# Inverting each chunk's triangular blocks alone, in blocks of 16, with the merge to 32 on TensorE

## Chip, cores, metric

One core of a Trainium2 chip, FP32 data. The metric is the device time of one execution in microseconds. Durations below come from one profiled execution of the kernel before.

## What is computed

The input is r, k, v, w, a, b for 4 batches, 8 heads, 768 time steps and 40 features. A recurrence with a 40 by 40 state per batch and head gives y:

```python
for t in range(S):
    y[:, :, t] = einsum('bhd,bhde->bhe', rt, state)
    Sa = einsum('bhde,bhe->bhd', state, at)
    state_decay = state * wt[:, :, None, :] - einsum('bhd,bhe->bhde', Sa, bt)
    state = state_decay + einsum('bhd,bhe->bhde', vt, kt)
```

y, reshaped to 3072 tokens of 320 features, goes into a mixture of 8 experts: logits of a gate, eight rounds of row and column normalization, and the weighted sum over the experts of `relu(x @ w1[e]) @ w2[e]` with 1024 hidden features.

## The kernel before, in words

**Chunks.** The 768 steps are cut into 12 chunks c of 64, for each of 4 batches b. The heads go in 4 pairs. Within a chunk the recurrence becomes products with a 64 by 64 unit triangular matrix per batch and head that has to be inverted: 32 matrices a chunk. Each is cut into two diagonal blocks of 32 by 32 (so 64 blocks a chunk) and one block off the diagonal.

**prep(c, b)** (L107 to L165) loads `inp` (L109), scans the decays on DVE into q (L114) and g (L122), forms kb and ab on POOL or DVE (L133, L139, L140), and multiplies and transposes them on PE into ll (L145) and kt (L153). Results go into one of 17 prepared sets: sx, bb, g, cc. ll's lower half goes to DRAM as `ld` (L148, L164). Each set lies in a memory pool of its own, and some sets that are not yet in use serve as input buffers in the first eight preparations.

**Inversion.** GROUPS pairs the chunks. For two chunks at a time `load_lu` fetches 128 blocks of 32 by 32 (L342), one a partition, and DVE inverts them in place: `inv_diag` for i = 1 to 7 on the four 8 by 8 blocks of each (L170, L173), then `inv_off` with contractions of up to 2048 elements (L179, L182). `finish` transposes a copy (L331) and stores both to DRAM as `ud` and `nd` (L333, L334).

**Merge to 64.** `tload(c)` fetches blocks of the inverses as td and tt (L211, L213, L217) and of ld as lg (L208). `tmat` makes the block off the diagonal: gp on PE (L226), copies on ACT (L227, L228), op on PE (L231), copies on ACT (L232, L233) into tt.

**recur(c, b)** has five steps: av and its mask f (L251, L252); xc and copies x1, c1 on ACT (L259, L265, L266); pu = tt times x1 and its mask pm (L270, L272); c2, ws, y and z (L277, L279, L281, L292); the transposition zt and the copies vz for the next chunk (L297, L299, L300). y is stored for the experts as xd (L285), and the gate's product lp (L307) follows some steps later. The chain from chunk to chunk of one batch is f, xc, pu, c2, z, zt, vz.

**The experts.** After the attention, layer 1 (L545), sums on DVE (L563), relu on ACT (L566), a low part on DVE (L569) and layer 2 (L610) run in blocks. `prep_w` (L473 to L501) loads weights `ws` and splits them into wh and wl on ACT and POOL; `prep_x` (L508 to L533) loads tokens `xs` and makes xch and xcl on DVE and ACT. From the eighth block on the order is written by hand.

**What sets the order.** The attention's steps are collected in a list `ev` with due times (five a chunk, batches 1.1 apart) and called in that order; P0, PD, T_LEAD, L_LEAD and INV_DT place the preparations, the inversion and the merge in it. A scheduler then arranges each engine's instructions by these priorities, their dependences and the buffers in the pools. Each engine and each DMA queue works in its order. Nearly all DMAs are issued by SP.

Of the kernel before, what the change touches and what calls it, by code (L numbers as in the profile page):

```python
# [28 lines left out]
def attention(ctx, tc, d, xd, ps, pq, pt, gs, lg):  # L29
    nc = tc.nc  # L30
    pin = ctx.enter_context(tc.tile_pool(name="a_in", bufs=1))
    inv = ctx.enter_context(tc.tile_pool(name="a_inv", bufs=1))
# [15 lines left out]
    sx_b, bb_b, g_b, cc_b = ([None] * NSX for _ in range(4))
    raws = {}
    for n in range(NCH * NB - NSX, NCH * NB):  # L50
        i, pool = n % NSX, sets[n - NCH * NB + NSX]
        if i in IN_SETS or i in KB_SETS:
            raw = pool.tile([128, 1508], F32, name=f"st{i}")
            raws[i] = raw
            sx_b[i] = raw[0:R2, 0:832].rearrange("r (p h x) -> r p h x", h=2, x=104)
            bb_b[i] = raw[:, 832:1248].rearrange("r (p x) -> r p x", x=104)
            g_b[i] = raw[0:R2, 1248:1504].rearrange("r (p x) -> r p x", x=64)
            cc_b[i] = raw[0:R2, 1504:1508]
            continue
        sx_b[i] = pool.tile([R2, NP, 2, 104], F32, name=f"sx{i}")  # L60
        bb_b[i] = pool.tile([128, NP, 104], F32, name=f"bb{i}")
        g_b[i] = pool.tile([R2, NP, 64], F32, name=f"g{i}")
        cc_b[i] = pool.tile([R2, NP], F32, name=f"cc{i}")
# [746 lines left out]
```

## Time and profile before

| | us |
|---|---|
| time, median of 3 runs (lowest, highest) | 1882.25 (1881.03, 1883.9) |
| span of the profiled execution | 1888.6 |
| PE busy in it | 1768.8 |
| first pu of chunk 0 | 119.55 |
| last pu of chunk 11 starts | 556.95 |
| PE busy from 120 to 563 | 405.31 |
| PE busy from 600 to 1888 | 1279.82 |

A row of the timeline gives start, duration, engine, line, operation, output and inputs, and in brackets how long the engine was idle before and what ended it. A row of the groups gives line, engine, operation, shapes and count, then busy time and mean duration in ns, then idle time before and what ended it. PE rows count passes: an FP32 product of 4 matmuls shows as x8.

### The profile page before, as it was taken

How to read it: one execution, taken by the hardware profiler on the slowest of the kernel's cores; microseconds unless marked ns; L12 is line 12 of the kernel's file. 1: busy time of each engine (PE TensorE's matmuls, PEld its weight loads, DVE VectorE, ACT ScalarE, POOL GpSimd, SP SyncE). 2: the span in 40 equal slices, each digit the busy share in tenths (PEclk: the TensorE clock that was granted, in tenths of full speed). 3: DMA queues.
4: the chain of work that ended last, by engine and by line, in shares of the span. 5: the costliest groups of instructions: out<-in, count | busy, mean ns of one | idle time of the engine just before them, and what ended most of it. 6: DMA issues, size and time to landing. Idle time of an engine off the chain costs nothing.

```text
span 1888.6 us, 31821 instructions
## 1 busy us (share of the span) xinstructions
PE 1768.8 (94%) x12035; PEld 1731.0 (92%) x12035; DVE 1397.3 (74%) x2330; ACT 854.1 (45%) x1845; POOL 876.9 (46%) x845
## 2 busy tenths in 40 slices
PE   4468989899898999999999999999999999999999
PEld 4367888889888999999999999999999999999999
DVE  7767767696579877776867777886776767777676
ACT  5346656665563444343433434345343433434342
POOL 6535445542255255371835528004462826537170
PEclk8569968988899999999999999999999999999999
DMA  8567766865642011110201102111110201111011
GB/s 191 100 133 151 151 140 134 166 137 119 147 117 70 23 51 37 37 56 19 73 21 53 52 22 74 55 33 37 37 55 19 73 19 55 37 37 56 18 37 42
DMA packets 187838, 136.26 MB, mean 72 GB/s; under 512 B 155941, under 2 KB 165285, under 8 KB 187685
## 3 DMA queue, kind: packets, MB, share of 16 engines
q1 hardware_dynamic: 184485, 128.98, 27.8%
q10 hardware_dynamic: 3200, 5.25, 1.1%
q8 instruction: 95, 1.56, 0.4%
q14 instruction: 58, 0.48, 0.1%
HBM read 113.74 MB, written 20.45 MB: 71 GB/s over the span
## 4 chain that ended last, share of the span: by engine, by line
PE 76%; DVE 7%; issue 2%; DMA 2%; POOL 1%; ACT 1%; SPq 0%; DVEq 0%; POOLq 0%; ACTq 0%
PE op L610 35%; PE p L545 32%; PE xc L259 2%; PE pu L270 1%; PE av L251 1%; PE ll L145 1%; PE c L277 1%; PE lp L307 1%; PE gp L226 1%; PE op L231 1%; DVE hl L569 1%; DVE un L182 1%; DVE gt L182 1%; PE zt L297 0%; DMA rb<-in_r_dram 0%
## 5 line engine op out<-in xcount | busy, mean ns | idle before, releaser
L545 PE MATMUL p<-xch,wh 128*128 128x384 f32 (+1 forms) x1792 | 605.0, 339 | 5.2 <-DVE cs L654 1.8
L566 ACT ACTIVATE hh<-sm 128x384 fp32r<-128x384 f32 x512 | 269.5, 526 | 726.5 <-DVE sm L563 726.5
L610 PE MATMUL op<-wh,hh 128*128 128x320 f32 x1536 | 477.4, 311 | 1.0 <-ACT hh L566 0.9
L610 PE MATMUL op<-wl,hh 128*128 128x320 f32 x1536 | 474.9, 310 | 0.0
L610 PE MATMUL op<-wh,hl 128*128 128x320 f32 x1536 | 468.1, 310 | 4.4 <-DVE hl L569 4.3
L491 POOL TENSOR_TENSOR wl<-ws,wh 128x640 fp32r<-128x640 f32 x60 | 103.3, 1721 | 608.4 <-ACT wh L489 608.2
L569 DVE SCALAR_TENSOR_TENSOR hl<-sm,hh 128x384 fp32r<-128x384 f32 x512 | 370.9, 758 | 2.8 <-ACT hh L566 2.5
L545 PEld LDWEIGHTS p<-xch,wh 128*128 128x128 f32 (+1 forms) x1792 | 337.5, 188 | 8.5 <-DVE u L563 2.7
L545 PE MATMUL p<-xcl,wh 128*128 128x384 f32 x896 | 302.8, 338 | 0.0
L545 PE MATMUL p<-xch,wl 128*128 128x384 f32 x896 | 302.2, 337 | 0.0
L610 PEld LDWEIGHTS op<-wh,hh 128*128 128x128 f32 x1536 | 290.6, 189 | 1.6 <-ACT hh L566 1.5
L610 PEld LDWEIGHTS op<-wh,hl 128*128 128x128 f32 x1536 | 287.2, 188 | 5.4 <-DVE hl L569 5.2
L610 PEld LDWEIGHTS op<-wl,hh 128*128 128x128 f32 x1536 | 291.5, 190 | 0.0
L563 DVE TENSOR_TENSOR sm<-p,u 128x384 f32<-128x384 f32 x384 | 232.8, 616 | 9.2 <-PE p L545 0.4
L545 PEld LDWEIGHTS p<-xcl,wh 128*128 128x128 f32 x896 | 168.8, 188 | 0.0
L545 PEld LDWEIGHTS p<-xch,wl 128*128 128x128 f32 x896 | 168.7, 188 | 0.0
L563 DVE TENSOR_TENSOR sm<-p,p 128x384 f32<-128x384 f32 x128 | 71.3, 557 | 130.1 <-PE p L545 76.3
L563 DVE TENSOR_TENSOR p<-p,p 128x384 f32<-128x384 f32 x128 | 71.2, 556 | 101.6 <-PE p L545 101.1
L563 DVE TENSOR_TENSOR u<-p,p 128x384 f32<-128x384 f32 x128 | 70.9, 554 | 59.3 <-PE p L545 58.0
L145 PE MATMUL ll<-ab,kb 104*128 104x128 f32 x336 | 63.4, 348 | 46.8 <-POOL ab L140 20.9
L499 POOL TENSOR_TENSOR wl<-ss,wh 128x512 fp32r<-128x512 f32 x60 | 90.7, 1512 | 33.5 <-ACT wh L496 29.3
L145 PEld LDWEIGHTS ll<-ab,kb 104*128 104x128 f32 x336 | 55.1, 249 | 51.3 <-POOL ab L140 27.1
(161 smaller groups left out, 2825.1 us busy)
## 6 DMA issues: line engine op xcount, KB each, us to landing
ws<-in_wts_dram SPq DMA_DIRECT2D x60, 832.0 KB
inp<-in_inp_dram SPq DMA_DIRECT2D x42, 521.6 KB
rb<-in_r_dram SPq DMA_DIRECT2D x48, 208.0 KB
ld<-lt ACTq DMA_DIRECT2D x40, 128.0 KB
vz<-in_v_dram SPq DMA_DIRECT2D x48, 104.0 KB
f<-in_vt_dram SPq DMA_DIRECT2D x48, 80.0 KB
xd<-y SPq DMA_DIRECT2D x96, 40.0 KB
st<-in_inp_dram SPq DMA_DIRECT2D x6, 521.6 KB
```

Of the source, the lines that this page charges most:

```text
L145: nc.tensor.matmul(ll[:, p], lhsT=kb[:, p], rhs=ab[:, p], start=True, stop=True)
L182: nc.vector.tensor_reduce(out=dst, in_=prv.rearrange("u c k r -> u c r k"), op=ALU.add, axis=AX.X)
L226: nc.tensor.matmul(gp[:, p], lhsT=lb[:, p], rhs=t1[:, p], start=True, stop=True)
L231: nc.tensor.matmul(op[:, p], lhsT=gs[:, p], rhs=t2[:, p], start=True, stop=True)
L259: nc.tensor.matmul(xc[h][:, p], lhsT=pp["sx"][:, p, h], rhs=f[:, p, h], start=True, stop=True)
L491: g.tensor_tensor(out=wl[:, 0:640], in0=raw[:, 256:896], in1=wh[:, 0:640], op=ALU.subtract)
L499: g.tensor_tensor(out=lv[:, 3:7], in0=so[:, :, 0], in1=hv[:, 3:7, 0], op=ALU.subtract)
L545: nc.tensor.matmul(o, lhsT=w_, rhs=x_, start=(j == 0), stop=(j == 3))
L563: eng.tensor_tensor(out=out, in0=x, in1=y, op=ALU.add)
L566: nc.scalar.activation(out=hh[:, f, h], in_=sm[f][:, h], func=AF.Relu)
L569: v.scalar_tensor_tensor(out=hl[:, f, h], in0=sm[f][:, h], scalar=0.0, in1=hh[:, f, h], op0=ALU.max, op1=ALU.subtract)
L610: nc.tensor.matmul(ops[i], lhsT=a[:, h, cs], rhs=w_[:, cw], start=(f == 0 and h == 0 and j == 0), stop=(last and h == 1 and j == 2))
```

## The change

Each chunk is inverted by itself, a 16 by 16 block at a time. A chunk has 128 such blocks, one a partition, so `load_lu` makes two DMAs (L182), `inv_diag` works on two 8 by 8 blocks (L159, L162), and `inv_off` is two contractions of 512 elements (L166, L169). `store_un(c)` stores the inverses and a copy that ACT transposes (`tr`) to DRAM in rows of 16 (L196), loads cl (L187), cb (L198), ca (L200) and xt (L202), and expands cl and cb on POOL to block-diagonal operands bl and bu of 128 by 8 by 128, by a product with the mask `mask_m` (bu of chunk 0 on DVE). `merge(c)` multiplies on PE: 8 products g16 (L214), a copy gg on ACT, 8 products x16 (L219), a copy on ACT into xt, two transpositions y16 (L224), a copy xx on ACT, and stores to nd (L221) and ud (L228). `tload` and `tmat` work as before.

The prepared sets are 13 in one pool. There are four input buffers of 1029 columns where there were two of 1284 besides the borrowed sets: g is scanned backwards over the same decays as q, so the second copy of the decays falls away. lt goes to DRAM in rows of 64 (L143). Other pieces of `prep`'s memory get two buffers. P0 goes from -8 to -2.5, PD from 0.75 to 1.25, and I_LAG = 0.5 and M_LAG = 0.6 place the inversion and the merge. What runs after the attention is not edited; its line numbers fall by two.

The core of the diff:

```diff
-    sets = [ctx.enter_context(tc.tile_pool(name=f"a_set{i}", bufs=1)) for i in range(NSX)]
+    sets = ctx.enter_context(tc.tile_pool(name="a_set", bufs=1))
...
-    INV = [(inv_diag, (i,)) for i in range(1, 8)] + [(inv_off, a) for a in ((0, 8, 8), (16, 8, 8), (0, 16, 8))]
+    def inv_off(i):
+        gt = gtf.rearrange("u (c r) -> u c r", r=8)
+        if i == 0:
+            contract(gt, un[:, 0:8, 0:8], lu[:, 0:8, 8:16])
+        else:
+            contract(un[:, 0:8, 8:16], gt, un[:, 8:16, 8:16])
+
+    INV = [(inv_diag, i) for i in range(1, 8)] + [(inv_off, 0), (inv_off, 1)]
+
+    def load_lu(c):
+        for j in range(2):
+            nc.sync.dma_start(out=lu[j * 64:j * 64 + 64], in_=dap(lds[c], j * 1040, (2080, 64), (64, 16), (1, 16)))
+
+    def store_un(c):
+        ud, nd = ud_b[c % 2], nd_b[c % 2]
+        cl = inv.tile([128, 128], F32, name="cl")
+        nc.sync.dma_start(out=cl, in_=dap(lds[c], 16, (64, 16), (2080, 64), (1, 16)))
+        bl = inv.tile([128, 8, 128], F32, name="bl")
+        mk = mask_m.unsqueeze(1).broadcast_to([128, 128, 8])
+        nc.gpsimd.tensor_tensor(out=bl.rearrange("k g (s m) -> k (g s) m", m=8),
+                                in0=cl.unsqueeze(2).broadcast_to([128, 128, 8]), in1=mk, op=ALU.mult)
+        tr = inv.tile([128, 16, 16], F32, name="tr")
+        nc.scalar.copy(out=tr, in_=un.rearrange("u c s -> u s c"))
+        for t, x in ((ud, un), (nd, tr)):
+            for j in range(2):
+                nc.sync.dma_start(out=dap(t, j * 528, (1024, 64), (32, 16), (1, 16)), in_=x[j * 64:j * 64 + 64])
+        cb = inv.tile([128, 128], F32, name="cb")
+        nc.sync.dma_start(out=cb, in_=dap(ud, 528, (32, 16), (1024, 64), (1, 16)))
+        ca = inv.tile([128, 8, 16], F32, name="ca")
+        nc.sync.dma_start(out=ca, in_=dap(nd, 0, (32, 16), (1024, 64), (1, 16)))
+        xt = inv.tile([128, 8, 32], F32, name="xt")
+        nc.sync.dma_start(out=xt[:, :, 16:32], in_=dap(nd, 528, (32, 16), (1024, 64), (1, 16)))
+        bu = inv.tile([128, 8, 128], F32, name="bu")
+        (nc.vector if c == 0 else nc.gpsimd).tensor_tensor(
+            out=bu.rearrange("k g (s m) -> k (g s) m", m=8),
+            in0=cb.unsqueeze(2).broadcast_to([128, 128, 8]), in1=mk, op=ALU.mult)
+        mops[c] = (bl, ca, bu, xt)
+
+    def merge(c):
+        ud, nd = ud_b[c % 2], nd_b[c % 2]
+        bl, ca, bu, xt = mops[c]
+        gp = pt.tile([128, 8, 16], F32, name="g16", tag="pt")
+        for g in range(8):
+            nc.tensor.matmul(gp[:, g], lhsT=bl[:, g], rhs=ca[:, g], start=True, stop=True)
+        gg = inv.tile([128, 8, 16], F32, name="gg")
+        nc.scalar.copy(out=gg, in_=gp)
+        xp = pt.tile([128, 8, 16], F32, name="x16", tag="pt")
+        for g in range(8):
+            nc.tensor.matmul(xp[:, g], lhsT=bu[:, g], rhs=gg[:, g], start=True, stop=True)
+        nc.scalar.copy(out=xt[:, :, 0:16], in_=xp)
+        nc.sync.dma_start(out=dap(nd, 512, (32, 16), (1024, 64), (1, 16)), in_=xt[:, :, 0:16])
+        xq = pt.tile([128, 2, 128], F32, name="y16", tag="pt")
+        for i in range(2):
+            nc.tensor.transpose(xq[:, i], xt[:, 4 * i:4 * i + 4].rearrange("a g c -> a (g c)"), ident)
+        xx = inv.tile([128, 2, 8, 16], F32, name="xx")
+        nc.scalar.copy(out=xx, in_=xq.rearrange("a i (s m) -> a i m s", m=8))
+        for i in range(2):
+            nc.sync.dma_start(out=dap(ud, i * 4096 + 16, (32, 128), (8192, 8), (1, 16)), in_=xx[:, i])
...
-P0 = -8
-PD = 0.75
+P0 = -2.5
+PD = 1.25
+I_LAG = 0.5
+M_LAG = 0.6
...
-NSX = 17
+NSX = 13
+NIN = 4
```

How the order of instructions moves, at three places. A row names line, operation, output and inputs with a buffer's number, shape and count.

On PE, before the first pu (pu_880) of the kernel before:

```order
L226 MATMUL gp_756<-td_192,lg_193 64x32 x8
L145 MATMUL ll_906<-ab0_194,kb_896 128x128 x4
L153 MATMUL kt_911<-cst_144,kb_896 128x104 x4
L231 MATMUL op_767<-td_192,lg_193 64x32 x8
L226 MATMUL gp_949<-td_192,lg_193 64x32 x8
L270 MATMUL pu_880<-x1_863,tt0_190 128x104 x4
```

and of the changed kernel (pu_799; g16_362 to y16_384 are the merge of chunk 0, g16_591 to y16_613 that of chunk 1):

```order
L214 MATMUL g16_362<-ca_356,bl_346 128x16 x8
L147 MATMUL kt_778<-cst_98,kb_761 128x104 x4
L141 MATMUL ll_898<-ab0_156,kb_888 128x128 x4
L219 MATMUL x16_373<-gg_371,bu_360 128x16 x8
L147 MATMUL kt_905<-cst_98,kb_888 128x104 x4
L224 MATMUL y16_384<-cst_98,xt_358 128x128 x2
L214 MATMUL g16_591<-ca_552,bl_542 128x16 x8
L219 MATMUL x16_602<-gg_600,bu_556 128x16 x8
L224 MATMUL y16_613<-cst_98,xt_554 128x128 x2
L256 MATMUL gp_674<-td_154,lg_155 64x32 x8
L261 MATMUL op_685<-td_154,lg_155 64x32 x8
L256 MATMUL gp_841<-td_154,lg_155 64x32 x8
```

The row after the last one is pu_799. Two merges stand ahead of it, and ll_898 is the thirteenth ll of the program, where ll_906 is the seventeenth.

On PE, where chunk 2 begins (pu_1731 is its first pu) in the kernel before:

```order
L251 MATMUL av_1705<-rb_1699,vz4_201 104x128 x4
L297 MATMUL zt_1711<-cst_144,z_1595 40x104 x4
L307 MATMUL lp_1775<-gs_65,y_1377 64x8 x2
L145 MATMUL ll_1611<-ab1_195,kb_1603 128x128 x4
L153 MATMUL kt_1616<-cst_144,kb_1603 128x104 x4
L277 MATMUL c2_1718<-pm_1644,bb7_178 104x104 x4
L270 MATMUL pu_1731<-x1_1693,tt0_190 128x104 x4
```

and in the changed kernel (pu_1740, four rows behind these; g16_1381 to y16_1403 are the merge of chunk 3, gp_1565 and op_1576 belong to chunk 2):

```order
L307 MATMUL c2_1715<-pm_1642,bb7_120 104x104 x4
L214 MATMUL g16_1381<-ca_1337,bl_1327 128x16 x8
L219 MATMUL x16_1392<-gg_1390,bu_1341 128x16 x8
L224 MATMUL y16_1403<-cst_98,xt_1339 128x128 x2
L337 MATMUL lp_1434<-gs_65,y_1034 64x8 x4
L337 MATMUL lp_1525<-gs_65,y_1151 64x8 x4
L256 MATMUL gp_1565<-td_154,lg_155 64x32 x8
L141 MATMUL ll_1601<-ab0_156,kb_1593 128x128 x4
L147 MATMUL kt_1608<-cst_98,kb_1593 128x104 x4
L261 MATMUL op_1576<-td_154,lg_155 64x32 x8
```

The merge of chunk 3 stands in one piece between the last c2 of chunk 1 and gp of chunk 2.

On DVE, the last gate copies (lg) and the first operands of the experts (xcl0, xch0) in the kernel before:

```order
L525 TENSOR_TENSOR xcl0_5550<-xs_5594,xch0_5549 128x3x128
L528 TENSOR_TENSOR xch0_5549<-xs_5594,xch0_5549 32x3x128
...
L312 COPY lg_62<-lp_5221 64x8
L531 TENSOR_TENSOR xcl0_5550<-xt_5600,xch0_5549 128x4x128
L533 TENSOR_TENSOR xch0_5549<-xt_5600,xch0_5549 32x4x128
```

and in the changed kernel (lp_6007 is the last gate product, mxs the first step behind it):

```order
L342 COPY lg_62<-lp_6007 64x8
L624 TENSOR_REDUCE mxs_6199<-lg_62 128x1
L523 TENSOR_TENSOR xcl0_6057<-xs_6101,xch0_6056 128x3x128
L526 TENSOR_TENSOR xch0_6056<-xs_6101,xch0_6056 32x3x128
L529 TENSOR_TENSOR xcl0_6057<-xt_6107,xch0_6056 128x4x128
L531 TENSOR_TENSOR xch0_6056<-xt_6107,xch0_6056 32x4x128
L523 TENSOR_TENSOR xcl0_6057<-xs_6119,xch0_6056 128x3x128
```

Before, all twelve such instructions on xcl0 and xch0 stand ahead of the last seven gate copies. Now the first of them stands behind the last gate copy. The same holds for the first cast of wh0 on ACT (before among chunk 10's and 11's copies, now behind the last x1 and c1) and for the first wl0 on POOL (now behind the last y).

More of the change, by code (lines that the diff above doesn't have):

```diff
@@ L37, in attention @@
     dr = ctx.enter_context(tc.tile_pool(name="a_dr", bufs=2, space=bass.MemoryType.DRAM))
-    cst = const.tile([128, 64 + 64 + 104 + 128 + 40 + 260], F32, name="cst")
+    dr1 = ctx.enter_context(tc.tile_pool(name="a_dr1", bufs=1, space=bass.MemoryType.DRAM))
+    cst = const.tile([128, 668], F32, name="cst")
     nc.sync.dma_start(out=cst, in_=d["cst"])
@@ L45, in attention @@
     one65 = cst[0:R2, 400:660]
+    mask_m = cst[:, 660:668]
     NTB = 2
[L48 to L63, printed above, removed]
+    sx_b = [sets.tile([R2, NP, 2, 104], F32, name=f"sx{i}") for i in range(NSX)]
+    bb_b = [sets.tile([128, NP, 104], F32, name=f"bb{i}") for i in range(NSX)]
+    g_b = [sets.tile([R2, NP, 65], F32, name=f"g{i}") for i in range(NSX)]
+    cc_b = [sets.tile([R2, NP], F32, name=f"cc{i}") for i in range(NSX)]
     tt_b = [const.tile([128, 4 * NP, 128], F32, name=f"tt{i}") for i in range(NTB)]
@@ new lines, in merge @@
+    def merge(c):
[16 more added lines that the diff above has]
+        nc.scalar.copy(out=xx, in_=xq.rearrange("a i (s m) -> a i m s", m=8))
+        for i in range(2):
+            nc.sync.dma_start(out=dap(ud, i * 4096 + 16, (32, 128), (8192, 8), (1, 16)), in_=xx[:, i])
@@ L365, in attention @@
             ev.append((t + 2 * SKEW * half, tmat, (c, half)))
-    for s, cs in enumerate(GROUPS):
-        us = slice(0, 64 * len(cs))
-        t0 = 5 * cs[0] - 10
-        n = len(cs) * NB
-        for i in range(n):
-            cb = (cs[0] + i // NB, i % NB)
-            j = cb[0] * NB + cb[1] - NSX
+        for b in range(NB):
+            j = c * NB + b - NSX
             t = 5 * (j // 4) + 3 + SKEW * (j % 4) + 0.01
-            t = max(t, t0 + P0 + PD * i) if s else -20 + 0.01 * i
-            ev.append((t, do_prep, (s,) + cb + (i == 0,)))
-        t += 0.02
-        ev.append((t, load_lu, (s, len(cs))))
+            t = max(t, 5 * (c - 2) + P0 + PD * b) if c else -20 + 0.01 * b
+            ev.append((t, prep, (c, b)))
+        t += 0.02 if c == 0 else I_LAG
+        ev.append((t, load_lu, (c,)))
         for i, (fn, a) in enumerate(INV):
-            ev.append((t + INV_DT * i, fn, (us,) + a))
-        ev.append((t + INV_DT * 10 + 0.01, finish, (s, us)))
+            ev.append((t + INV_DT * i, fn, (a,)))
+        ev.append((t + INV_DT * 9, store_un, (c,)))
+        ev.append((t + INV_DT * 9 + M_LAG * (c > 0), merge, (c,)))
     for _, fn, args in sorted(ev, key=lambda x: x[0]):
@@ L398 @@
 NRB = 2
[L399 to L403 removed]
+KB_POOL = (1, 2, 3, 4, 5, 6, 7)
 N_SP = 8
[L405 removed]
 NFAST = 6
@@ L777, in _layout @@
     gate[0:40], gate[64:104] = wg[0], wg[1]
-    cst = np.zeros((128, 660), np.float32)
+    cst = np.zeros((128, 668), np.float32)
     i = np.arange(64)
@@ L788, in _layout @@
     cst[64:104, 360:400] = np.eye(40)
-    cst[:, 400::65] = 1.0
+    cst[:, 400:660:65] = 1.0
+    cst[:, 660:668] = np.tile(np.eye(8), (16, 1))
     arrays = dict(inp=inp, r=rb.reshape(NCH, NB, R2, NP, 128), v=packed(g["v"]),
```

162 lines of the change are left out of this document (56 added, 106 removed).

## Prediction

> **What bounds the kernel now.** I read the page first, then the table by stretches, then the timeline at the start, at a chunk's edge and at the handover to the experts. The page gives the frame:
>
> ```profile
> span 1888.6 us, 31821 instructions
> PE 1768.8 (94%) x12035; PEld 1731.0 (92%) x12035; DVE 1397.3 (74%) x2330; ACT 854.1 (45%) x1845; POOL 876.9 (46%) x845
> ```
>
> The profiled execution lasted 1888.6 us from first to last instruction, 6.35 us above the median of 1882.25 of the three timed runs (1881.03 to 1883.9). I sum against 1888.6 and take 6.35 off at the end. About 0.2%, or 3.8 us, is what a measurement of this kernel can tell from no change.
>
> The stretches (columns: the stretch, its length, busy time of PE, weight loads, DVE, ACT and POOL with instruction counts, then granted clock, DMA share, GB/s; three answers):
>
> ```profile
> 0.00:120.00 120.00, 52.39 (x286) 47.18 (x287) 84.41 (x128) 52.32 (x130) 64.78 (x88) 0.65 0.73 147
> 120.00:563.00 443.00, 405.31 (x3563) 378.30 (x3563) 324.90 (x503) 266.80 (x662) 202.55 (x231) 0.87 0.67 140
> ```
> ```profile
> 563.00:600.00 37.00, 31.29 (x172) 29.25 (x172) 35.55 (x49) 18.03 (x34) 29.43 (x26) 0.91 0.29 90
> 600.00:1888.00 1288.00, 1279.82 (x8021) 1276.25 (x8019) 952.41 (x1652) 516.95 (x1021) 580.10 (x500) 1.00 0.13 41
> ```
>
> From 600 on PE is busy 1279.82 of 1288 us at clock 1.00 with code that the change leaves alone, so that part stays. The change acts on three others. In 0 to 120 PE is idle more than half the time, waiting for the first inversion. In 120 to 563 PE is busy 405.31 of 443 us: 37.7 us idle. A granted clock of 0.87, if it is a mixture of 1.0 and 0.5, means 26% of the time, 115 us, at half, which costs some 57 us more. In 563 to 600 DVE is the fullest engine, 35.55 of 37.
>
> **The start.** The timeline (start, duration, engine, line, operation; single rows):
>
> ```profile
> 50.54 0.69 DVE L122 TENSOR_TENSOR_SCAN st<-inp,g 104x256 f32<-104x256 f32 x1
> ...
> 58.60 0.17 DVE L170 TENSOR_TENSOR pr<-un,lu 128x4 f32<-128x4 f32 x1 [1.43 <-DMA lu<-ld]
> ...
> 96.39 3.80 DVE L182 TENSOR_REDUCE un<-pr 128x128 f32<-128x2048 f32 x1
> ```
> ```profile
> 100.22 1.10 SPq L333 DMA_DIRECT2D ud<-un  x2
> ```
> ```profile
> 108.44 1.78 PE L226 MATMUL gp<-td,lg 64*64 64x32 f32 x15 [1.65 <-DMA td<-nd]
> ```
> ```profile
> 119.55 2.03 PE L270 MATMUL pu<-x,tt 128*128 128x104 f32 x8 [3.38 <-ACT tt L233]
> ```
>
> Chunks 0 and 1 are inverted together from 58.60 to 100.2, and the first pu runs at 119.55, 19.3 us later: store, load, gp, op, tt. The new kernel inverts chunk 0 alone. The order puts its first inversion instruction behind ten g scans; the tenth of before is the one at 50.54, so I start at 50, perhaps 46 with four smaller input buffers. Its own work is some 7 us (below), and about 6 us of scans and masks stand between: end at 60. Then come one more DRAM round trip (8.2 us, from the stores at 100.22 to gp at 108.44), bu (2.3, below) and the merge with its copies at half clock (5), and after that the old 19.3: 95, so **25 us earlier** (15 if the second chunk's inversion gets in between, 35 if the preparation packs tighter).
>
> **The inversions on DVE.** Groups on DVE, 0 to 640 (last columns: busy, mean ns, idle before):
>
> ```profile
> L182 DVE TENSOR_REDUCE un<-pr 128x64 f32<-128x512 f32 (+2 forms) x24 | 47.9, 1994 | 0.1
> L182 DVE TENSOR_REDUCE gt<-pr 128x64 f32<-128x512 f32 (+2 forms) x24 | 45.9, 1911 | 0.1
> ...
> L179 DVE TENSOR_TENSOR pr<-un,lu 128x512 f32<-128x512 f32 (+2 forms) x24 | 30.1, 1256 | 0.1
> L179 DVE TENSOR_TENSOR pr<-gt,un 128x512 f32<-128x512 f32 (+2 forms) x24 | 29.9, 1248 | 0.1
> ...
> L170 DVE TENSOR_TENSOR pr<-un,lu 128x4 f32<-128x4 f32 (+6 forms) x42 | 15.6, 371 | 9.2 <-DMA lu<-ld 4.1 <-DMA tt<-ud 2.2 <-DMA ld<-lt 1.9
> L173 DVE TENSOR_REDUCE un<-pr 128x4 f32<-128x4 f32 (+6 forms) x42 | 9.9, 235 | 1.0
> ```
>
> ```profile
> L182 DVE TENSOR_REDUCE gt<-pr 128x64 f32<-128x512 f32 x12 | 12.9, 1073 | 0.1
> ...
> L179 DVE TENSOR_TENSOR pr<-un,lu 128x512 f32<-128x512 f32 x12 | 9.2, 762 | 0.1
> ```
>
> The first six (a group's name shows one of its forms) sum to 179.3 us in six segments, 30 us each. The last two keep forms apart: a contraction of 512 elements is 0.76 + 1.07. What is left per chunk is two of these, 3.7 us, and 14 short instructions on half the blocks, at most 7 times 0.371 + 0.235, which I put at 3.5: 7 us, 86 in all, in pieces of 7 instead of 30. What this is worth shows at a chunk's edge. PE at chunks 4 and 5:
>
> ```profile
> 263.37 1.06 PE L270 MATMUL pu<-x,tt 128*128 128x104 f32 x8
> ...
> 271.38 1.19 PE L226 MATMUL gp<-td,lg 64*64 64x32 f32 x16 [1.40 <-DMA td<-nd]
> ...
> 279.26 2.04 PE L270 MATMUL pu<-x,tt 128*128 128x104 f32 x8
> ```
> ```profile
> 307.64 1.06 PE L270 MATMUL pu<-x,tt 128*128 128x104 f32 x8
> 318.75 1.06 PE L270 MATMUL pu<-x,tt 128*128 128x104 f32 x8
> ```
>
> From the last pu of chunk 3 to the first of chunk 4, whose inversion has just ended, pass 15.9 us, with gp waiting for td; from chunk 4 to 5, inverted together with it, 11.1. The 4.8 us come at five edges (chunks 2, 4, 6, 8, 10): 24. PE's zt row, 120 to 563, has 3.5 us of waits for DVE besides:
>
> ```profile
> L297 PE MATMUL zt<-cst,z 104*40 104x104 f32 x176 | 26.0, 274 | 9.1 <-POOL z L292 5.6 <-DVE z L292 1.9 <-DVE un L173 1.6
> ```
>
> Together **DVE's relief is -28**. Its bounds are 0 (PE then waits for the merge there) and -95 (all 37.7 idle and 57 of clock).
>
> **The merge on PE.** Per chunk 16 products of 128 by 128 weights with 16 columns and two transposes. The warm pu at 263.37 (x8 for four FP32 products: two passes each) took 1.06 us, 0.133 a pass, with full weights and 104 columns. An lp, with half the weight columns and 8 columns of data:
>
> ```profile
> 556.35 0.67 PE L307 MATMUL lp<-gs,y 104*64 104x8 f32 x9
> ```
>
> That is 0.074 a pass. The merge has pu's weights, so I take 0.122, near pu: 32 passes are 3.9, the transposes 0.3, together 4.2 a chunk (2.6 to 4.8). Ten merges lie behind the first pu, where PE is 91% busy: **+42** (26 to 48). The Trainium skill (TensorE: Matmul & The Clock Gate, LDWEIGHTS) has a weight load cost its columns over 1.2 ns, 107 ns for 128, whatever the product's width; by that the passes are 3.4 a chunk and the term 37. No row here has so narrow a product; pu's 0.133 with 104 columns does not speak against it.
>
> The merge is a chain: g16, ACT copy, x16, ACT copy, y16. In several chunks the order stands these three back to back. A copy behind gp:
>
> ```profile
> 272.60 0.36 ACT L227 COPY lg<-gp 32x256 f32<-32x256 f32 x1 [0.51 <-PE gp L226]
> ```
>
> 0.36 and a hop of about as much, twice, is 1.4 us in the half of the chunks where nothing stands between: **+8** (0 to 14).
>
> **Fewer sets.** 13 preparations instead of 17 stand ahead of the first pu, so four more fall beside the recurrence. Groups on PE, 325 to 352, three preparations at clock 0.94:
>
> ```profile
> L145 PE MATMUL ll<-ab,kb 104*128 104x128 f32 x24 | 3.4, 284 | 0.5 <-POOL ab L140 0.5
> ...
> L153 PE MATMUL kt<-cst,kb 104*128 104x104 f32 x12 | 1.6, 253 | 0.0
> ```
>
> (3.4+1.6)/3 is 1.6 each: **+6**.
>
> **POOL and ACT** get bl, bu and four copies a chunk. The nearest row on POOL:
>
> ```profile
> L133 POOL TENSOR_TENSOR kb<-inp,q 104x512 f32<-104x512 f32 x40 | 51.1, 1279 | 54.2 <-PE kt L153 30.3 <-DVE q L114 11.7 <-issue 6.3
> ```
>
> Twice that width at 1.28 is 2.3 to 2.6 us each, 5 a chunk on an engine busy 202.55 of 443: nothing, as long as z does not stand behind it; 2.5 a chunk (+27) if it always did. ACT has 266.80 of 443 and gets 1.7 a chunk: nothing. The reversed g scan has 260 elements for 256: nothing.
>
> **The handover.** The experts' first operands are prepared on DVE, ACT and POOL. Before, part of that stands among the last chunks' steps, and PE begins products early:
>
> ```profile
> 538.80 0.61 PE L545 MATMUL p<-xch,wh 128*128 128x384 f32 x2
> ```
>
> In the new order all casts of wh0, wl0 on POOL and the x0 operands on DVE stand behind the attention's last instruction, because their memory now lies where late sets live. Groups on DVE, 0 to 640, six uses each:
>
> ```profile
> L533 DVE TENSOR_TENSOR xch<-xt,xch 32x512 fp32r<-32x512 f32 x6 | 7.5, 1245 | 0.1
> L528 DVE TENSOR_TENSOR xch<-xs,xch 32x384 fp32r<-32x384 f32 x6 | 6.1, 1024 | 0.1
> L531 DVE TENSOR_TENSOR xcl<-xt,xch 128x512 fp32r<-128x512 f32 x6 | 5.2, 872 | 0.1
> L525 DVE TENSOR_TENSOR xcl<-xs,xch 128x384 fp32r<-128x384 f32 x6 | 4.9, 815 | 0.0
> ```
>
> Three of the six are x0's: 11.9 us, and with the sums ahead of two of them 15, all moved into the stretch that DVE bounds: **+15** (8 to 20; PE has little else to do there).
>
> **The sum.** -25 +42 +8 +6 -28 +15 = +18: 1906.6 in a profile, **1900 us** as a median.
>
> **Rivals.** *Faster.* DVE's short segments let PE run without pauses, and the clock recovers. For it: 57 us of half clock. Against it: the merge adds pauses of its own. The start gains 30, relief 48, the hops cost 3, the handover 8: -30+42+3+6-48+8 = -19, **1863**. The Trainium skill (same page, the clock gate) says that the array falls to half after a window of about 3.4 us without work; the 1.5 us gaps of the rows above would not do that, the longer ones at the edges would; the rows agree with a pu of 2.04 us right behind such an edge. *Slower: transfers.* DMA rows, 0 to 620 and for 116 to 120:
>
> ```profile
> q1 hardware_dynamic: 170757, 76.94, 59.5%
> ```
> ```profile
> DMA packets 3080, 0.40 MB, mean 100 GB/s; under 512 B 3071, under 2 KB 3071, under 8 KB 3080
> ```
>
> In those 4 us all engines were full, so 770 short packets a microsecond is the rate. Per chunk the change moves 13,312 pieces of 64 B (2,048 replace pieces of 128 B) and 2,048 of 256 B where 256 of 2 KB were: 13,000 more, 17 us of full engines beside 27 (0.67 of the 40 of a chunk, 39.5 from 279.26 to 318.75), less some 2 for smaller inputs: 42 us, longer than a chunk now takes. SP issues 11 DMAs more a chunk and stands in order:
>
> ```profile
> SPq L285 <- POOL y L281: 54.4, 28, 4.5
> SPq L242 <- PE xc L259: 34.1, 16, 6.3
> ```
>
> If the loads of cb, ca and xt come late, g16 of chunk c+1, which stands ahead of gp of chunk c, holds PE. It decides when the DMA share of 120 to 550 passes 0.9; at 4 us in each of 11 chunks above my sum: **1944**. The Trainium skill (DMA: Bandwidth & Descriptors, Specifications) puts full rate at 512 B or more and has shorter pieces read, modified and written; if the 7,168 written pieces of 64 B a chunk took twice their time for it, that would be 9 us more and lead here. No row above shows such a penalty. *No change:* start and relief just pay the merge, 1882; the sum's terms are uncertain by 10 to 20 each, so this is a thin slice. That a stage is skipped can be excluded: all twelve merges stand in PE's order.
>
> **Chances.** My forecast (1886 to 1920) 0.38; slower by transfers 0.20; faster 0.34; same 0.08. Faster 0.34, same 0.08, slower 0.58. The range for eight in ten goes from 1862 to 1940: the faster rival's price and nearly that of the slower one.
>
> **What would show it.** First pu near 95; g16, x16 and y16 4.2 us a chunk; the edges of even and odd chunks alike; 42 to 43 us between first pus of chunks 1 to 8; the first wh0 cast behind the last x1 copy and the 563-to-600 picture 15 us later against the last pu. I am wrong if PE's idle time and half clock in the recurrence fall by more than the merge costs, or if SP or the transfers set the chunk's length.

## The result and the profile after

The changed kernel took 2000.97 us (median of 4 runs, 1987.79 to 2013.28) beside 1883.08 for the kernel before on the same chip: a ratio of 1.0596 (1.0532 to 1.066). It is slower, as forecast, but by 118 us and not by 18, and outside the range. The profiled execution lasted 1991.8 us, 103.2 more than that of before. The page of the changed kernel (TensorE's granted clock last, in tenths, 40 slices):

```profile
span 1991.8 us, 32870 instructions
PE 1871.7 (94%) x12443; PEld 1825.8 (92%) x12443; DVE 1324.4 (66%) x2361; ACT 870.7 (44%) x1889; POOL 877.0 (44%) x865
PEclk8598678686858799999999999999999999999999
```

DVE's load fell from 1397.3 to 1324.4 us as meant, and PE's rose from 1768.8 to 1871.7: by as much as the whole time. The stretches are cut at the first pu, the last pu and where the experts run undisturbed (columns as in the prediction):

```profile
0.00:99.00 99.00, 59.22 (x304) 53.84 (x304) 72.15 (x137) 44.39 (x109) 52.82 (x75) 0.67 0.78 147
99.00:633.00 534.00, 491.95 (x3899) 460.68 (x3898) 242.30 (x495) 279.20 (x705) 190.43 (x240) 0.77 0.57 108
633.00:690.00 57.00, 27.94 (x137) 22.97 (x138) 41.71 (x56) 22.11 (x38) 42.42 (x40) 0.73 0.28 86
690.00:1991.00 1301.00, 1292.58 (x8108) 1288.28 (x8106) 968.28 (x1676) 524.96 (x1038) 591.38 (x510) 1.00 0.13 42
```

The experts keep clock 1.00. The recurrence, 443 us at clock 0.87 before, takes 534 at 0.77, though DVE has 242 us to do in it where it had 325. DMA is less busy than before (0.57 for 0.67). The three terms, from the starts of pu in the timelines:

| | before | after | difference |
|---|---|---|---|
| span's start to first pu | 119.6 | 99.1 | -20.4 |
| first pu to last pu (the recurrence) | 437.4 | 533.8 | +96.4 |
| last pu to the span's end | 1331.7 | 1358.9 | +27.2 |

A chunk's edge, from the last pu of chunk 4 to the first of chunk 5, on PE:

```profile
307.49 1.14 PE L300 MATMUL pu<-x,tt 128*128 128x104 f32 x8 [1.08 <-ACT c L296]
...
311.19 0.97 PE L307 MATMUL c<-pm,bb 128*104 128x104 f32 x8
314.06 1.96 PE L214 MATMUL g<-ca,bl 128*128 128x16 f32 x16 [1.91 <-DMA ca<-nd]
316.47 3.03 PE L219 MATMUL x<-gg,bu 128*128 128x16 f32 x16 [0.45 <-ACT gg L216]
319.85 0.69 PE L224 MATMUL y<-cst,xt 128*128 128x128 f32 x2 [0.36 <-ACT xt L220]
320.47 1.88 PE L337 MATMUL lp<-gs,y 104*64 104x8 f32 x16
322.28 1.91 PE L256 MATMUL gp<-td,lg 64*64 64x32 f32 x16
325.18 2.08 PE L141 MATMUL ll<-ab,kb 104*128 104x128 f32 x8 [0.99 <-POOL ab L136]
...
327.88 1.91 PE L261 MATMUL op<-td,lg 64*64 64x32 f32 x16
...
333.24 1.49 PE L300 MATMUL pu<-x,tt 128*128 128x104 f32 x8
```

From pu to pu 25.8 us pass; before, the longest such edge had 15.9. PE is idle for some 4 us of it. The rest is the merge of chunk 6 (g16, x16, y16) and what follows it, from 317 on at up to double duration. gp took 1.19 us at chunk 4 of before, here 1.91; an ll takes 2.08, where e1_late below has 1.08. The 11 edges sum to 211.6 us (126.8 before); the steps within the 12 chunks, from a chunk's first pu to its last, sum to 322.2 (310.6).

The trace also records when TensorE's granted clock changes. Each of the ten merges behind the first pu is followed, 0.8 to 4.4 us after its first g16, by a stretch at half clock, which lasts 3.4 to 47.8 us. Only one other such stretch begins in the recurrence, at 610.6, and it lasts 3.4 us.

### The profile page after: what moved, and what is told of

The parts are those of the page before. It is cut to its first block, busy times and chain, and to the rows that moved or that the text cites. A ratio compares the mean times of both kernels' runs of the same rounds, so it can differ in the third digit from the quotient of the medians.

```text
span 1991.8 us, 32870 instructions
## 1 busy us (share of the span) xinstructions
PE 1871.7 (94%) x12443; PEld 1825.8 (92%) x12443; DVE 1324.4 (66%) x2361; ACT 870.7 (44%) x1889; POOL 877.0 (44%) x865
## 4 chain that ended last, share of the span: by engine, by line
PE 73%; DVE 4%; DMA 3%; issue 1%; ACT 1%; POOL 1%; SPq 0%; ACTq 0%; DVEq 0%; POOLq 0%
PE op L608 33%; PE p L543 31%; PE xc L289 1%; PE lp L337 1%; PE pu L300 1%; PE c L307 1%; PE av L281 1%; DMA ca<-nd 1%; PE x L219 1%; DMA nd<-tr 1%; PE ll L141 1%; PE op L261 1%; PE g L214 1%; PE gp L256 1%; DVE sm L561 0%
## 5 line engine op out<-in xcount | busy, mean ns | idle before, releaser
L141 PE MATMUL ll<-ab,kb 104*128 104x128 f32 x384 | 76.8, 364 | 41.8 <-DVE ab L136 11.6
L141 PEld LDWEIGHTS ll<-ab,kb 104*128 104x128 f32 x384 | 67.5, 264 | 46.2 <-POOL ab L136 16.9
```

Source lines behind the costliest of these rows:

```text
L141: nc.tensor.matmul(ll[:, p], lhsT=kb[:, p], rhs=ab[:, p], start=True, stop=True)
```

## The experiments

Theories, as the expectations name them. **P**, the place: the merge stands in one piece ahead of gp, so all of it lies on the path between two chunks. **W**, the passes: narrow products cost PE their time wherever they stand. **T**, transfers: the short pieces and SP's queue delay ca, cb and xt. **C**, the clock: narrow products keep TensorE at half clock, and wider ones would lift it. Times are read by the ratio to the kernel before on the same chip.

**First: which part.** e1_late and e3_pools change one thing each, e4_pq the PSUM buffers of g16, x16 and y16; e2_nomerge takes the products away and keeps every transfer.

```diff
e1_late
-M_LAG = 0.6
+M_LAG = 5.0
e2_nomerge (g16, x16, y16 and their copies go; these stay)
+        nc.scalar.copy(out=xt[:, :, 0:16], in_=ca)
+        nc.scalar.copy(out=xx.rearrange("a i m s -> a (i m s)"), in_=bl[:, 0:2].rearrange("a g s -> a (g s)"))
e3_pools (sx, bb, g and cc of set i then come from sets[i])
-    sets = ctx.enter_context(tc.tile_pool(name="a_set", bufs=1))
+    sets = [ctx.enter_context(tc.tile_pool(name=f"a_set{i}", bufs=1)) for i in range(NSX)]
+    sets = {n % NSX: sets[n - NCH * NB + NSX] for n in range(NCH * NB - NSX, NCH * NB)}
e4_pq (so for all three)
-        gp = pt.tile([128, 8, 16], F32, name="g16", tag="pt")
+        gp = pq.tile([128, 8, 16], F32, name="g16", tag="pq")
```

> The changed kernel with M_LAG 5.0 instead of 0.6, so that the merge of a chunk comes due some four steps later: in PE's order g16, x16 and y16 then stand in the middle of the chunk before, with pu, xc, zt and ll between them, and no longer in one piece ahead of the next chunk's gp. Theory P (the place of the merge costs the time: PE stands in it at a chunk's edge, at half clock, and gp, the preparations and the gate products wait behind): the edges, last pu of a chunk to first pu of the next, fall from 18.5 us in the mean to 11 to 13, the time falls by 60 to 80 us against the changed kernel, to about 1925. Theory W (the merge's own passes on PE cost it, wherever they stand): the time falls by less than 20. Theory T (the short transfers set the pace): no change, 2001 within 15.

> The changed kernel without the merge's 16 products and two transpositions on PE and without the copy gg; the two other ACT copies read ca and bl instead, and all transfers and POOL's products stay. So the inverse of 32 is not formed. Theory P: the time falls by the edges' stretching and by the passes, 80 to 110 us, to 1890 to 1920. Theory W: it falls by 40 to 50, the price of ten merges. Theory T: it stays near 2001, since every transfer is still there.

> The changed kernel with one memory pool for each of the 13 prepared sets, ordered by last use, as the kernel before had them; on DVE the first operands of the experts then stand ahead of the last seven gate copies again. If the handover is what the last 25 us of the loss are (first pu of chunk 11 to the end: 1377 against 1352), the time falls by 20 to 25 and that stretch is back at 1352 to 1357; if it is a consequence of the slower recurrence, it stays. Theories P, W and T say the same of the rest: the recurrence does not move.

> The changed kernel with g16, x16 and y16 in the PSUM buffers of ll and kt (pq) instead of those of gp, op and lp (pt). If the part of theory P is true that the merge holds up the gate's products by the two pt buffers, and with them y, and behind y on POOL the z of the recurrence, the waits of POOL's y for lp (63 us) and DVE's for lp (92 us) fall to less than half and the time by 20 to 40. If it is only the standing of PE, the time moves by less than 10, since the merge stays at the edge in one piece. Theory T: no change.

Measured: e1_late 1938.35 us, 1.0262 (1.0219 to 1.0305); e2_nomerge 1888.21, 0.999 (0.9957 to 1.0022); e3_pools 1987.73, 1.0516 (1.045 to 1.0582); e4_pq 2019.12, 1.0688 (1.064 to 1.0736).

Without the products the kernel is as fast as before, with every transfer of the change in it. So **T is refuted** as what sets the pace, and everything else in the change sums to nothing. The products on PE are the whole loss. The recurrence of e2_nomerge:

```profile
90.00:519.00 429.00, 406.85 (x3557) 375.89 (x3557) 247.90 (x513) 276.37 (x695) 191.16 (x241) 0.88 0.74 135
```

This run can't show what the products themselves wait for. In the changed kernel that is a small part, g16's wait for the load of ca (total, times and longest, 99 to 633):

```profile
PE g L214 <- DMA ca<-nd: 12.1, 7, 3.4
```

Moving the merge later, by one number, brings back over half of the loss. PE in e1_late (single rows; the same merge, now among the steps of a chunk):

```profile
315.28 1.11 PE L261 MATMUL op<-td,lg 64*64 64x32 f32 x16
316.32 2.43 PE L214 MATMUL g<-ca,bl 128*128 128x16 f32 x16
318.59 1.16 PE L300 MATMUL pu<-x,tt 128*128 128x104 f32 x4
319.55 2.98 PE L289 MATMUL xc<-f,sx 104*104 104x104 f32 x16
...
322.75 3.43 PE L219 MATMUL x<-gg,bu 128*128 128x16 f32 x16
...
330.49 0.63 PE L224 MATMUL y<-cst,xt 128*128 128x128 f32 x2
...
338.40 1.08 PE L141 MATMUL ll<-ab,kb 104*128 104x128 f32 x8
```

g16, x16 and y16 stand apart, with pu, xc, av and ll of other batches between them, and no product waits for ca. The edges sum to 120.7 us, below before's 126.8; the steps within the chunks grow from 310.6 to 355.7, by 45 us, or 4.1 for each of the 11 merges that now lie behind the first pu. That is close to the 4.2 the prediction gave the passes, but near half of it is clock by the split below. So it is **P for the larger part, W for the rest**. e4_pq shortened the waits for lp's buffer (DVE's 91 us to 53) and was no faster: these buffers are not what holds the edge.

**Second: place and pools together, and the start alone.** b1_late_pools and b2_late6_pools are e3_pools with M_LAG = 5.0 and 6.0, e5_nomerge_pools is e2_nomerge with e3's pools, and g1_groups is the kernel before with one line changed.

```diff
g1_groups
-GROUPS = [[0, 1], [2, 3], [4, 5], [6, 7], [8, 9], [10, 11]]
+GROUPS = [[0], [1, 2], [3, 4], [5, 6], [7, 8], [9, 10], [11]]
```

> Both edits of the second and the third run: M_LAG 5.0 and one memory pool for each set. Theory P left 1938 with M_LAG alone, where the last pu to the end takes 1363 us against 1332 before. If the handover's loss is the sets' memory, this stretch comes back to 1332 to 1345 and the time to 1908 to 1922, that is 1.01 to 1.02 of the kernel before; what remains is then the merge's passes, some 45 us, less what the start gains. If the memory is not the cause, the time stays at 1930 to 1945.

> As the run before it, but M_LAG 6.0: g16, x16 and y16 stand another step later, between the third and the fourth pu of the chunk before, with gp and op of the same chunk long done. By theory P the place within a chunk does not matter any more once other products stand between: within 10 us of the run before it. If lead time to the next tload matters, it is slower by 10 to 30, with PE waiting for td at the edges.

> Without the merge's products on PE (the inverse of 32 is not formed, as in the second run) and with one pool for each set. The run without the merge was even with the kernel before: 29 us earlier at the start, 9 us shorter in the recurrence and 33 us longer from the last pu to the end. If those 33 are the sets' memory, this one is at 0.98 to 0.99 of the kernel before, with 1332 to 1345 from the last pu to the end; if not, it stays even.

> The kernel before with another grouping: chunk 0 is inverted alone, then chunks 1 and 2 and so on in pairs, the last one alone. No merge on PE, blocks of 32, 17 sets. It does the part of the change that shortens the start. The first pu comes at 97 to 104 instead of 119.6, since four preparations fewer lie ahead of the first inversion; a seventh inversion of 30 us on DVE costs up to 5. The time is 10 to 20 us below that of the kernel before, 0.99. If DVE's extra segment eats it, no difference.

Measured: b1_late_pools 1936.41, 1.0253 (1.0199 to 1.0307); b2_late6_pools 1914.14, 1.014 (1.0078 to 1.0202); e5_nomerge_pools 1879.62, 0.9943 (0.9914 to 0.9971); g1_groups 1911.53, 1.012 (1.0052 to 1.0188).

The pools bring 0.8% over the change as it is, 0.1% in b1 over e1, 0.5% in e5 over e2 and 1.3% in b2 over m6_late (below): some 13 us, with intervals as wide. e5 is below before only because it leaves the products out. They act at the end (last pu to end 1340.1 in e3_pools for 1358.9). b1 missed the 1908 to 1922 expected of it, although that stretch came back to 1342.5; b2, expected within 10 us of b1, was 22 faster. b2_late6_pools is the best version of the change in full precision, and still 1.4% slower than before. g1_groups has its first pu at 105.1, 14.5 earlier than before, and loses it again: the edge from chunk 0 to 1 takes 22.5 us, and the recurrence has 163 us at half clock for 115. An earlier start that costs a seventh inversion on DVE is no gain here.

**Third: is it the clock?** If products of 16 columns starve the clock, the same weights with 64 columns should lift it. w1_wide_merge repeats the columns of g16 and x16 four times; w2_wide_all does it for gp, op and lp as well (64 columns each); w3_late6_wide is that on b2_late6_pools; v1_before_wide widens gp, op and lp of the kernel before. Only the first copy of each result is used.

```diff
w1_wide_merge (x16 alike)
-        gp = pt.tile([128, 8, 16], F32, name="g16", tag="pt")
+        gp = pt.tile([128, 8, 4, 16], F32, name="g16", tag="pt")
-            nc.tensor.matmul(gp[:, g], lhsT=bl[:, g], rhs=ca[:, g], start=True, stop=True)
+            nc.tensor.matmul(gp[:, g], lhsT=bl[:, g], rhs=ca[:, g].unsqueeze(1).broadcast_to([128, 4, 16]), start=True, stop=True)
```

> The changed kernel with every product of g16 and x16 made 64 columns wide instead of 16, by reading the same 16 columns four times into PSUM; only the first copy is used. The traces show that the clock of a window of 3.41 us goes with the number of columns that PE streamed in the window before (1752 or more: full, fewer: half; right in 94 of 100 of 1543 windows of nine traces), and not with PE's idle time. Theory C (the merge's narrow products starve that count, and half clock stretches the edge): with 1024 columns in place of 256 in each of g16 and x16, the half-clock time, 246 us of the recurrence, falls by a fifth to a third and the time by 15 to 50. Theory I (idle gaps decide the clock): no change, or a few us slower.

> As the run before it, and gp and op 64 columns wide instead of 32, and the gate's lp 64 instead of 8, by the same repetition. The edge's sequence g16, x16, y16, lp, gp, op stays in one piece in the order. Theory C: the half-clock time falls to less than 120 us of the recurrence and the time by 50 to 90 us, to 1910 to 1950, although PE has just as many passes. Theory I: no change.

> M_LAG 6.0, one pool for each set, and all narrow products 64 wide. Without the widening it took 1.014 of the kernel before, at clock 0.88 in the recurrence. Theory C: clock 0.95 or more there, the time falls by 15 to 30 to about 0.998 to 1.006 of the kernel before. Theory I: it stays at 1.014.

> The kernel before, not the changed one, with gp and op 64 columns wide instead of 32 and lp 64 instead of 8. It has 114 us at half clock in its recurrence. Theory C: at least a third of these go, the time falls by 12 to 30 us, to 0.985 to 0.994 of the kernel before. Theory I: no change within 0.3%.

Measured: w1_wide_merge 2018.79, 1.0677 (1.0612 to 1.0742); w2_wide_all 1986.24, 1.0533 (1.048 to 1.0587); w3_late6_wide 1912.11, 1.0149 (1.0099 to 1.0199); v1_before_wide 1896.51, 1.0061 (1.0037 to 1.0085).

No gain beyond the intervals anywhere: **C's prediction of the time fell.** The recurrence of b2_late6_pools and of w3_late6_wide:

```profile
95.00:565.00 470.00, 439.62 (x3934) 415.91 (x3934) 254.18 (x505) 287.00 (x720) 196.97 (x249) 0.88 0.67 126
```
```profile
95.00:563.00 468.00, 430.49 (x3936) 398.30 (x3935) 256.71 (x502) 286.94 (x719) 201.85 (x252) 0.92 0.66 127
```

In w3 the clock did rise, from 0.88 to 0.92, and the stretch is 2 us shorter: more columns cost about what the clock gave.

**Fourth: the passes doubled.** Each of the 16 products is made twice, in b2_late6_pools (d1_double_mid) and in the changed kernel (d2_double_edge); m6_late is M_LAG = 6.0 alone.

```diff
d1_double_mid, d2_double_edge (g16 and x16)
-        for g in range(8):
+        for g in (*range(8), *range(8)):
m6_late
-M_LAG = 0.6
+M_LAG = 6.0
```

> M_LAG 6.0 and one pool for each set (1.014 of the kernel before), with each of the 16 products of g16 and x16 issued twice into the same place. This adds 3.9 us of passes a chunk where other work stands between. If PE's passes are the price of the merge there, the time rises by 35 to 50 us, to 1.033 to 1.041 of the kernel before. If PE has slack, by less than 20.

> The changed kernel with each of the 16 products of g16 and x16 issued twice, all at the edge as it has them. Theory P (at the edge everything stands behind the merge, and PE works there at half clock): each pass costs double, the time rises by 60 to 95 us against the changed kernel, to about 2060 to 2095. Theory W (a pass costs the same anywhere): by 35 to 50, as in the run before it.

> The changed kernel with M_LAG 6.0 alone. If the place makes the difference to 1914 and the pools bring little, 1915 to 1930; if the pools bring the 20 us, 1935 to 1945, where M_LAG 5.0 stood.

Measured: d1_double_mid 2047.7, 1.0864 (1.0802 to 1.0927); d2_double_edge 2101.24, 1.1088 (1.1005 to 1.1171); m6_late 1938.06, 1.0268 (1.0215 to 1.0321).

Doubling costs 134 us among the steps and 100 at the edge (136 and 93 by the ratios), though at 4 us of passes a chunk it should be 45; 35 to 50 and 60 to 95 were expected. The recurrence of d1_double_mid and of d2_double_edge:

```profile
102.00:706.00 604.00, 581.80 (x4291) 549.47 (x4291) 262.43 (x514) 291.23 (x725) 210.25 (x259) 0.74 0.54 101
```
```profile
110.00:732.00 622.00, 571.57 (x4222) 541.04 (x4221) 241.15 (x495) 279.21 (x705) 189.19 (x239) 0.72 0.48 93
```

The clock is at 0.74 and 0.72. The trace's clock record splits the length: time at half clock is counted, and half of it taken off.

| | first to last pu | of it at half clock | counted at full clock |
|---|---|---|---|
| before | 437.4 | 115.1 | 379.8 |
| e2_nomerge | 428.4 | 102.4 | 377.2 |
| after | 533.8 | 241.8 | 412.9 |
| e1_late | 476.4 | 146.7 | 403.0 |
| b2_late6_pools | 469.8 | 111.4 | 414.1 |
| w3_late6_wide | 467.9 | 75.7 | 430.1 |
| d1_double_mid | 604.2 | 309.8 | 449.3 |
| d2_double_edge | 621.5 | 347.3 | 447.9 |

At full clock, doubling adds 35 us to the recurrence at either place (449.3 - 414.1, 447.9 - 412.9). That is 3.2 for each of the 11 merges behind the first pu in d1 and 3.5 for each of the 10 in d2, close to 32 passes at the 0.112 us from one pass to the next that the changed kernel shows at full clock. The other 99 and 53 us of the recurrence's growth (134 and 88) are time at half clock; in d2 the first pu also comes 11 us later. The same split of the merge itself, after against e2_nomerge: 36 us of work (412.9 - 377.2) and 70 us of half clock ((241.8 - 102.4) / 2). Put among the steps, e1_late: 26 and 22. So the place matters mostly by the clock that comes with it.

Taking half of the time at half clock off is an accounting, as if all of that time waited for PE. In the 63 runs of the kernel before, compared with others on the same chip, 1 us more at half clock went with 0.33 us more in all. At that rate the 70 us would be 46 and the work 59: the sizes of the two parts are estimates, their order is not settled.

**Fifth: the passes halved, and wide work beside them.** h1_r32 and h2_r32_edge make g16 and x16 in the one-pass form of FP32 with less precision (their rows count x96 passes for x192), on b2_late6_pools and on the changed kernel; ACT makes one more copy a chunk (cr of ca). c1_dummy puts two useless products of 512 columns ahead of each of g16, x16 and y16.

```diff
h1_r32, h2_r32_edge (bu and gg alike)
-        bl = inv.tile([128, 8, 128], F32, name="bl")
+        bl = inv.tile([128, 8, 128], F32R, name="bl")
+        cr = inv.tile([128, 8, 16], F32R, name="cr")
+        nc.scalar.copy(out=cr, in_=ca)
-            nc.tensor.matmul(gp[:, g], lhsT=bl[:, g], rhs=ca[:, g], start=True, stop=True)
+            nc.tensor.matmul(gp[:, g], lhsT=bl[:, g], rhs=cr[:, g], start=True, stop=True)
c1_dummy (ahead of x16 and y16 alike)
+        for _ in range(2):
+            nc.tensor.matmul(gp, lhsT=ca.rearrange("a g c -> a (g c)"), rhs=bl[:, 0:4], start=True, stop=True)
```

> The changed kernel with two useless products of 512 columns ahead of each of g16, x16 and y16, written into the same PSUM buffer before the real ones and overwritten. They read ca, gg or xt, so they stand with the merge at the edge. They add 2.6 us of PE work a chunk at full clock, 5.1 at half. Theory C (a window of 3.41 us in which PE streams less than about 1540 columns of 128 rows puts the next one at half clock; the merge starves it): the time at half clock in the recurrence falls from 242 us to 100 to 150 and pays for the work: 1955 to 1995. If half clock is only a companion of PE's standing: 2030 to 2060.

> M_LAG 6.0, one pool for each set (1.014 of the kernel before), and the merge's 16 products in the one-pass format fp32r: bl, bu, gg and a copy of ca are rounded to it, so that the block off the diagonal of each 32 has less precision. Half the narrow passes are gone. Doubling them cost 134 us; if the price of the narrow passes goes on downwards like that, 40 to 65 us are gained, to 0.98 to 0.993, faster than both kernels. If only their own time counts, 20 to 25: 1.001 to 1.004.

> The changed kernel with the merge's 16 products in fp32r, at the edge as it has them. Half of the narrow passes are gone. By the slope of the doubling (100 us for the same number of passes) 50 us are gained, to 1940 to 1960. If PE's standing at the edge is the cost and not the passes, less than 20.

Measured: c1_dummy 2055.35, 1.086 (1.0785 to 1.0935); h1_r32 1901.02, 1.0076 (1.0049 to 1.0102); h2_r32_edge 1970.39, 1.0413 (1.0344 to 1.0483).

Half the passes take 1.8% off at the edge, some 35 us, and 0.6% off among the steps, some 12 us, which is within the intervals. The expectations had 50 or under 20 at the edge and 20 to 65 among the steps; neither came true. Wide work beside the narrow products brings no time back: c1_dummy is 2.6% above the changed kernel. No complete version beats the kernel before.

The clock did answer to the wide work, though. A run's span and mean granted clock give its time at half clock in the whole execution, as (1 - clock) × 2 × span (the clock records hold only 1.0 and 0.5), and with half of that taken off the span, its time counted at full clock:

| | at half clock, us | counted at full clock, us |
|---|---|---|
| after (4 runs) | 334 to 386 | 1818 to 1822 |
| w1_wide_merge (4) | 353 to 432 | 1821 to 1827 |
| w2_wide_all (4) | 280 to 347 | 1823 to 1837 |
| c1_dummy (4) | 236 to 333 | 1911 to 1918 |
| b2_late6_pools (4) | 202 to 277 | 1788 to 1806 |
| w3_late6_wide (4) | 164 to 180 | 1825 to 1828 |

Against the kernel that each starts from, w2, w3 and c1 have less half clock. The extra columns cost about half of what that gives in w2 (whose 0.6% is within the intervals), as much in w3 and far more in c1.

## Why the prediction was wrong, point by point

**Direction and cause: right.** The time went up, and the merge on PE is what does it (0.999 without its products).

**The failed step: "Ten merges lie behind the first pu, where PE is 91% busy: +42", with +8 for the hops.** It priced the merge at the warm rate, as work beside the recurrence. The work was sized about right: at full clock a pass of the merge starts 0.112 us after the one before (0.213 at half; 0.122 forecast), and by the split above the products add 36 us in the changed kernel, 26 in e1_late. The prediction says that no row there is so narrow; its lp row, with 8 columns, is narrower, but loads 64 weight columns. w1's passes of 64 columns start 0.112 us apart as well. What the products cost is 105 us of recurrence (533.8 against 428.4), because of two things that the step left out. First, the order on record already showed the merge in one piece between the last c2 of chunk 1 and gp of chunk 2, and no step of the recurrence stands between the merge and the next pu in that edge's rows: what stands at an edge is on the path of all four batches. First pus of chunks 1 to 8 come 46 to 56 us apart, not 42 to 43. Moving the merge away takes 3.3% off, 63 us. Second, the clock falls with it. The prediction read 26% of half clock in before and let only the faster rival move it; it went from 115 to 242 us. How much of the 105 us is work and how much clock is known only as the estimates above. The merge's own groups on PE, 0 to 640 us:

```profile
L219 PE MATMUL x<-gg,bu 128*128 128x16 f32 x192 | 34.8, 328 | 1.8 <-ACT gg L216 1.8
L214 PE MATMUL g<-ca,bl 128*128 128x16 f32 x192 | 27.4, 286 | 15.2 <-DMA ca<-nd 15.0
L224 PE MATMUL y<-cst,xt 128*128 128x128 f32 x24 | 7.8, 425 | 3.3 <-ACT xt L220 3.3
```

70.0 us for 12 merges is 5.8 each, not 4.2. The hops were small: x16 waited 1.8 us for its copy in all and y16 3.3, against 8 forecast; what waits is g16 for ca, 15.0 us, which the sum had at nothing.

**Start, -25: right in kind, -20.4.** Without the merge's products it is -29.0 (first pu of e2_nomerge at 90.52). First pu of the changed kernel:

```profile
99.14 2.03 PE L300 MATMUL pu<-x,tt 128*128 128x104 f32 x8
```

**DVE's relief and fewer sets, -28 and +6: too large.** The sum was -22; e2_nomerge has a recurrence only 9 us shorter than before (428.4 for 437.4). The inversion on DVE, 0 to 640:

```profile
L159 DVE TENSOR_TENSOR pr<-un,lu 128x2 f32<-128x2 f32 (+6 forms) x84 | 40.4, 480 | 25.6 <-DMA lu<-ld 23.7
...
L162 DVE TENSOR_REDUCE un<-pr 128x2 f32<-128x2 f32 (+6 forms) x84 | 16.1, 192 | 2.6 <-DMA ud<-un 0.4
L169 DVE TENSOR_REDUCE gt<-pr 128x64 f32<-128x512 f32 x12 | 13.0, 1079 | 0.2
L169 DVE TENSOR_REDUCE un<-pr 128x64 f32<-128x512 f32 x12 | 12.9, 1072 | 0.2
L166 DVE TENSOR_TENSOR pr<-gt,un 128x512 f32<-128x512 f32 x12 | 11.9, 989 | 0.2
L166 DVE TENSOR_TENSOR pr<-un,lu 128x512 f32<-128x512 f32 x12 | 10.0, 834 | 0.2
```

They sum to 104 us, where 86 were forecast: the products of `inv_diag` took 480 ns each and not at most 371. The edges of even and odd chunks did become alike, but at 17 to 26 us (the second to the eighth), where before had 11 to 16.

**Handover, +15: +27.2.** The place was right: the first wh0 cast and the x0 operands come after the last pu (at 632.93), and PE waits 17.26 us for them (ACT, DVE and PE in time):

```profile
637.25 0.83 ACT L483 CAST wh<-ws 128x768 fp32r<-128x768 f32 x1 [4.97 <-POOL y L311]
641.94 1.53 DVE L523 TENSOR_TENSOR xcl<-xs,xch 128x384 fp32r<-128x384 f32 x1 [3.45 <-ACT xch L517]
655.17 1.01 PE L543 MATMUL p<-xch,wh 128*128 128x384 f32 x2 [17.26 <-ACT xch L517]
```

The first such product of before ran at 538.80, 18 us ahead of its last pu; this one comes 22 us behind. But DVE does not set the stretch, as the prediction had it: it is busy 41.71 of 57 us, POOL 42.42. Where the sets' memory comes free earlier (e3_pools), the stretch behind the last pu is 19 us shorter, though the last chunk itself then takes longer (34.6 us from its first to its last pu, for 18.1). The rest, some 16 to 23 us from chunk 11's first pu to the end against before (1368 to 1375 in four kernels with pools, 1351.8 before), was not taken apart.

The four terms as measured, -20.4 start, +105.4 merge, -9.0 relief and sets, +27.2 handover, make the 103.2 of the two profiles.

**Rivals.** *Transfers* did not set the pace: the DMA share fell, and its condition (0.9) was far off; the main queue, 0 to 620, moved 303,829 pieces for 170,757 in less of the time (56.0% for 59.5%):

```profile
q1 hardware_dynamic: 303829, 65.76, 56.0%
```

That share fell because the recurrence got longer. At e2_nomerge's pace, with a recurrence 9 us shorter than before's, it is 0.74 for 0.67: some 20 us more of full engines in the whole recurrence, where the prediction had 15 in each chunk. The rate of 770 pieces a microsecond did not carry over to these. Its price of 1944 was nearer by accident. The rule that the prediction cited from the Trainium skill (DMA: Bandwidth & Descriptors, Specifications), that pieces under 512 B are written by read and modify, shows no cost in the time here: e2_nomerge keeps them all at 0.999. *Faster by a recovering clock* had the sign wrong. It weighed the pauses that go, not the narrow work that comes. Its pauses of 3.4 us at the edges are not in the trace either: before's longest pause of PE between its first and last pu is 2.54 us, and the clock is at half for 115 us all the same. *POOL* shows no cost either: its products bl and bu, at 1.95 us each, are in e2_nomerge too.

## To carry to other kernels

When work moves onto the engine that bounds the kernel, find where the order puts it before it is priced: between the last step of one chunk and the first of the next, every microsecond is on the path of this kernel, and a due time later by most of a chunk brought back 63 of 118 us here. Price it at the clock of its place, not at the best row, and expect the neighbours to slow down with it. To split such a loss, take the products away and keep their transfers, move them, double them and halve them.

## What the runs showed of the hardware

PE at half clock while it is never idle. The changed kernel in the stretch from 570 to 600, and two rows of it:

```profile
570.00:600.00 30.00, 30.00 (x164) 26.96 (x164) 6.94 (x17) 8.08 (x21) 5.13 (x7) 0.50 0.47 135
```
```profile
570.31 2.04 PE L300 MATMUL pu<-x,tt 128*128 128x104 f32 x8
...
596.81 2.04 PE L300 MATMUL pu<-x,tt 128*128 128x104 f32 x8
```

Busy 30.00 of 30.00 us, clock 0.50 throughout, and pu at 2.04 us where 1.06 is its time at full clock. In the trace the clock changes in steps of 3.41 us, as the Trainium skill has it (TensorE: Matmul & The Clock Gate, What's actually happening). The Trainium skill (same page and section) lets the clock fall after an idle window and rise after a busy one; these rows differ, and the measurement decides. What fits is the amount streamed: for each pass its columns times its rows over 128, summed over a window of 3.41 us, with a pass that spans two windows divided between them. Above about 1,530 the next window had the full clock, below it half, in 99.6% of the 2,817 windows between the first and the last pu of 19 traces (all but c1_dummy's): in all 302 changes upward and 98% of the 284 downward. The threshold was fitted to these same windows. PE's busy time says it in 69% at best, and that the clock stays as it is in 79%. By this measure 16 columns with 128 by 128 weights fill PE's time and stream little. It is a rule read off the traces, for the stretch between the first and the last pu only, and not a shown cause. The runs that streamed more on purpose agree in part: the clock rose in w2, w3 and c1 and not in w1, and none of them gained time beyond its interval. At half clock w1's passes of 64 columns start 0.213 us apart, 16 a window, which makes 1,024: by the same rule not enough. Whether the half clock can be cured at a price below its worth stays open.
